# One decode step with cached attention: gate vectors in two halves, idle products over the whole array, and the softmax sums of a pair turned by a transposition

## The chip, the cores and the metric

The kernel runs on one core of a Trainium2 chip. The metric is device time in microseconds (us), as the median of repeated executions. A core has five engines that work side by side, each through its own queue of instructions in the order in which they were issued: TensorE (PE in the profile, its weight loads PEld), VectorE (DVE), ScalarE (ACT), GpSimd (POOL) and SyncE (SP, which here only issues transfers). Engines wait for one another through semaphores. Sixteen DMA engines move data between HBM and the on-chip memory SBUF; PE writes its results to PSUM.

## What is computed

One token goes through a block with adaptive layer norm: attention of one query over a cache, then a two-layer network with a squared ReLU.

```python
mod = (silu(c) @ w_mod).reshape(1, 6, 1, 640)        # c: (1, 640), w_mod: (640, 3840)
sa, ca, ga, sb, cb, gb = (mod[:, j] for j in range(6))
h = layernorm(x) * (1 + ca) + sa                      # x: (1, 1, 640)
q = (h @ wq).reshape(1, 1, 32, 192).transpose(0, 2, 1, 3)
scores = einsum("bhqd,bhkd->bhqk", q, k_cache) * 192 ** -0.5   # caches: (1, 32, 8192, 192)
o = einsum("bhqk,bhkd->bhqd", softmax(scores), v_cache)
x = x + ga * (o.reshape(1, 1, 6144) @ wo)
h = layernorm(x) * (1 + cb) + sb
x = x + gb * (relu(h @ w1 + b1) ** 2 @ w2 + b2)       # w1: (640, 1536), w2: (1536, 640)
```

Everything is in 32-bit floats. The two caches are 403 MB of the 452 MB that are read.

## The kernel before

**Slots and transfers.** SBUF has three large slots (`slot`), through which the caches and the weights pass in turn: for every head h the keys k (with the weights that the head's neighbours need behind them), then the values v. `load_k(h)` and `load_v(h)` stand at the top of the loop's pass over head h. SP issues a load as soon as the slot that it fills has been released: the keys of head h+1 go where the values of head h-1 were, the values of head h+1 where the keys of head h were. Behind the last values come `wm1_t` (the output weights of the last pair and three of the six modulation blocks), `w1_t` with the last modulation block `gb`, and `w2_t`, in the slots of the last heads.

**One head.** The 8192 positions lie 64 to each of 128 partitions. `keys` goes over the head's keys in two halves (head 31 in four quarters): DVE multiplies them by the query in place (L201), POOL adds part of the products in halves (L203), and DVE sums them to scores (L204, L205). After the first half, `between` issues either the query of the next pair (even heads) or the attention's output projection of the pair before (`attend`, odd heads). `softmax` takes the maximum over all positions, for which PE turns a column of 128 partial maxima (L220) and DVE reduces it (L222); ACT takes the exponential and, with it, the 128 partial sums of the head (L228), into a column of `sp`. `values` multiplies the probabilities with v on PE, in 24 products of 512 columns, three at a time, each in two passes (L240), into a PSUM tile of the tag "o".

**A pair of heads.** After an odd head's exponentials, `total` adds the partial sums of the pair's two heads over the partitions with a product by a matrix of ones (L97), which leaves the sums on every partition. `project(i - 1)` stands at the start of the odd head 2i+1: DVE takes the reciprocals (L213), then for each head of the pair picks the wanted entries out of the values' result, scaled by the reciprocal (L254), and adds them (L256); PE gathers the pair into one column (L258, `ps_oT`). `attend` later copies that to SBUF (L262, `oT`) and PE multiplies it by the output weights (L267, `att_a`; L272 for the last pair).

**The order.** The schedule is written by hand: each engine runs its instructions in the order of the program text. So on PE `project(i - 1)` stands behind the values of head 2i, and on DVE it stands ahead of `keys(2i + 1)`.

**Modulation.** `mod` computes blocks of the modulation on PE with the vector `e` (silu of c) repeated 32 times as the weights: for each of five blocks of rows four products (L140), one for each quarter of the 640 outputs, into the partitions of that quarter. So the result stands in 32 copies of 160 columns on each quarter of the partitions; DVE copies it to `mods` (L145). Block 2 (the gate `ga`) is computed between the softmax and the values of head 31, block 5 (the gate `gb`) after the first layer's product `ps_f` (L343).

**The tail.** `project(15)`, `attend(15)`, the residual `x1`, blocks 3 and 4 of the modulation, the layer norm, `ps_f`, the squared ReLU with its 32x32 transposition to `fT` (L82), block 5, the idle products `ps_warm` (L355), whose result nobody reads, and the second layer `ps_y` (L363), whose weights come in five pieces. DVE ends with the gate and the sum (L366, L367), and SP stores the result.

Of the kernel before, what the change touches and what calls it, by code (L numbers as in the profile page):

```python
# [8 lines left out]
F32 = mybir.dt.float32  # L9
AF = mybir.ActivationFunctionType  # L10
ALU = mybir.AluOpType
AX = mybir.AxisListType

P = 128
D = 640
# [4 lines left out]
G = 4  # L20
DG = D // G
FG = FF // G
KB = DG // 32
FB = FG // 32
PW = 2 * DH
E = 8
ED = 64
# [5 lines left out]
WO = 3 * D  # L33
# [12 lines left out]
def block_kernel(ctx: ExitStack, tc: tile.TileContext, kw, ky, vc, wm0, wm1, w1, gb, w2, out):  # L46
    nc = tc.nc
    const = ctx.enter_context(tc.tile_pool(name="const", bufs=1))
    strm = ctx.enter_context(tc.tile_pool(name="strm", bufs=3))
    work = ctx.enter_context(tc.tile_pool(name="work", bufs=2))  # L50
    psum = ctx.enter_context(tc.tile_pool(name="psum", bufs=1, space=bass.MemoryType.PSUM))
    ctx.enter_context(tc.manual_schedule())

    def slot(name):
        return strm.tile([P, SLOT], F32, tag="slot", name=name, bufs=3)


    ident = const.tile([P, P], F32, name="ident")
    make_identity(nc, ident)
    ones = const.tile([P, P], F32, name="ones")  # L60
    nc.vector.memset(ones, 1.0)

    mask = const.tile([P, E], F32, name="mask")
# [29 lines left out]
    def total(src, name):  # L93

        n = src.shape[1]
        ps = psum.tile([P, 512], F32, tag="sm", name="ps_" + name, bufs=2)
        nc.tensor.matmul(ps[:, :n], ones, src, start=True, stop=True)  # L97
        return ps[:, :n]
# [25 lines left out]
    e = const.tile([P, KB], F32, name="silu")  # L124
# [5 lines left out]
    mods = const.tile([P, 6, DG], F32, name="mods")  # L130

    def mod(first, n, w, steps=(KB,)):

        ps = psum.tile([P, 512], F32, tag="q", name=f"ps_mod{first}", bufs=2)
        b = 0
        for k in steps:
            for b in range(b, b + k):
                wb = w[:, b].rearrange("p (m n) -> p m n", m=n)
                for g in range(G):
                    nc.tensor.matmul(ps[32 * g:32 * (g + 1), :n * DG], e[:, b:b + 1].to_broadcast([P, 32]),  # L140
                                     wb[:, :, DG * g:DG * (g + 1)], start=(b == 0), stop=(b == KB - 1))
            b += 1
            if b < KB:
                yield
        nc.vector.tensor_copy(mods[:, first:first + n], ps[:, :n * DG].rearrange("p (m n) -> p m n", m=n))  # L145
        yield

    qb_t, k_t, v_t = {}, {}, {}

    def load(src, to, h, what):  # L150
# [6 lines left out]
    def load_k(h):  # L157

        load(kw[WITH_W.index(h)] if h in WITH_W else ky[WITHOUT_W.index(h)], k_t, h, "k")

    def load_v(h):
        load(vc[h], v_t, h, "v")
# [14 lines left out]
    def query(i, w):  # L177
        w = w.rearrange("p (b n) -> p b n", b=KB)
        ps = psum.tile([P, 512], F32, tag="q", name=f"ps_q{i}", bufs=2)
        for b in range(KB):  # L180
            nc.tensor.matmul(ps[:, :PW], hR[:, b], w[:, b], start=(b == 0), stop=(b == KB - 1))  # L181
        qb_t[i] = work.tile([P, PW], F32, name=f"qb{i}", tag="qb")
        nc.scalar.activation(qb_t[i], ps[:, :PW], AF.Copy, scale=DH ** -0.5)  # L183
# [24 lines left out]

    ri_t, ps_t, sum_t = {}, {}, {}

    def inverse(i):
        r = work.tile([P, 2], F32, tag="r", name=f"r{i}")
        nc.vector.reciprocal(r, sum_t.pop(i))  # L213
        ri_t[i] = r

    def softmax(h, sc):
        mp = work.tile([P, 1], F32, tag="mp", name=f"mp{h}")
        nc.vector.tensor_reduce(mp, sc, axis=AX.X, op=ALU.max)  # L218
        ps = psum.tile([P, 512], F32, tag="sm", name=f"ps_mx{h}", bufs=2)
        nc.tensor.transpose(ps[:, :P], mp.to_broadcast([P, P]), ident)  # L220
        nm = work.tile([P, 1], F32, tag="nm", name=f"nm{h}")
        nc.vector.tensor_reduce(nm, ps[:, :P], axis=AX.X, op=ALU.max, negate=True)  # L222

        p = work.tile([P, NPOS, 32 // E], F32, tag="p", name=f"p{h}", bufs=1)
        if h % 2 == 0:
            sum_t["part"] = work.tile([P, 2], F32, tag="sp", name=f"sp{h // 2}")
        sp = sum_t["part"]
        nc.scalar.activation(p, sc[:, :, None].to_broadcast([P, NPOS, 32 // E]), AF.Exp, bias=nm, accum_out=sp[:, h % 2:h % 2 + 1])  # L228
        if h % 2:
            sum_t[h // 2] = total(sp, f"sum{h // 2}")  # L230
        return p

    def values(h, p):
# [9 lines left out]
    os_t = {}  # L243

    def project(i):

        n = 32 * NV
        os_ = work.tile([P, 2, ED], F32, tag="os", name=f"os{i}")
        inverse(i)
        r2 = ri_t.pop(i)  # L250
        for a in range(2):
            h = 2 * i + a
            om = work.tile([P, ED, E], F32, tag="om", name=f"om{h}", bufs=1)
            nc.vector.scalar_tensor_tensor(om[:n], ps_t.pop(h)[:n].rearrange("p (d e) -> p d e", e=E), r2[:n, a:a + 1],  # L254
                                           mask[:n, None, :].to_broadcast([n, ED, E]), op0=ALU.mult, op1=ALU.mult)
            nc.vector.tensor_reduce(os_[:n, a], om[:n], axis=AX.X, op=ALU.add)  # L256
        os_t[i] = psum.tile([P, 512], F32, tag="sm", name=f"ps_oT{i}", bufs=2)
        nc.tensor.matmul(os_t[i][:, :n], os_[:n].rearrange("p a d -> p (a d)"), quad[:n], start=True, stop=True)  # L258

    def attend(i, w):  # L260
        oT = work.tile([P, 96], F32, tag="oT", name=f"oT{i}")
        nc.vector.tensor_copy(oT, os_t.pop(i)[:, :96])  # L262
        w = w.rearrange("p (j n) -> p j n", j=3)
        if i + 1 < NPAIR:
            for j in range(3):
                for g in range(2):
                    nc.tensor.matmul(att_a[32 * g:32 * (g + 1), :2 * DG], oT[:, 32 * j:32 * (j + 1)],  # L267
                                     w[:, j, 2 * DG * g:2 * DG * (g + 1)], start=(i == 0 and j == 0), stop=(i == NPAIR - 2 and j == 2))
            return
        for j in range(3):  # L270
            for g in range(G):
                nc.tensor.matmul(att_t[0][32 * g:32 * (g + 1), :DG], oT[:, 32 * j:32 * (j + 1)],  # L272
                                 w[:, j, DG * g:DG * (g + 1)], start=False, stop=(j == 2))

    def gather():

        nc.scalar.activation(att_s[:64], att_a[:64, :2 * DG], AF.Copy)
        att_t.append(psum.tile([P, 512], F32, tag="o", name="att", bufs=3))
        for g in range(G):
            nc.tensor.matmul(att_t[0][32 * g:32 * (g + 1), :DG], ident[:, 32 * (g // 2):32 * (g // 2) + 1].to_broadcast([P, 32]),  # L280
                             att_s[:, DG * (g % 2):DG * (g % 2 + 1)], start=True, stop=False)
# [3 lines left out]
    for h in range(H):  # L285
        i = h // 2
        if h:
            load_k(h)
        if h == H - 1:
            wm1_t = slot("wm1_t")  # L290
            nc.sync.dma_start(wm1_t[:, :WO + KB * D], wm1[:, :WO + KB * D])
        load_v(h)
        w = k_t[h][:, HD:]

        def between(c):
            if c == 0 and h % 2 and i:
                attend(i - 1, w)
            elif c == 0 and h % 2 == 0 and i + 1 < NPAIR:
                query(i + 1, w)
            elif c == 2 and h == H - 1:  # L300
                gather()

        if h % 2 and i:
            project(i - 1)
        sc = keys(h, between)
        p = softmax(h, sc)
        if h == H - 1:
            next(mod(2, 1, wm1_t[:, WO:WO + KB * D].rearrange("p (b n) -> p b n", b=KB)))
        values(h, p)


# [1 line left out]
    w1_t = slot("w1_t")  # L313
# [6 lines left out]
    gb_t = w1_t[:, KB * FF:KB * (FF + D)].rearrange("p (b n) -> p b n", b=KB)  # L320
    w1_t = w1_t[:, :KB * FF].rearrange("p (b n) -> p b n", b=KB)
    w2_t = w2_t[:, :FB * D].rearrange("p (b n) -> p b n", b=FB)

    project(NPAIR - 1)
    attend(NPAIR - 1, wm1_t[:, :WO])
    mod_b = mod(3, 2, wm1_t[:, WO + KB * D:WO + KB * 3 * D].rearrange("p (b n) -> p b n", b=KB), (2, 2, 1))
    next(mod_b)
# [13 lines left out]
    for b in range(KB):  # L341
        for g in range(G):
            nc.tensor.matmul(pf[32 * g:32 * (g + 1), :FG], hT2[:, b], w1_t[:, b, FG * g:FG * (g + 1)],  # L343
                             start=(b == 0), stop=(b == KB - 1))
    f = work.tile([P, FG], F32, name="f", tag="spread", bufs=1)
# [2 lines left out]
    nc.vector.tensor_mul(f, f, f)  # L348
    fT = columns(f, FG, "fT", work, tag="om", bufs=1)

    next(mod(5, 1, gb_t))
    idle = psum.tile([P, 512], F32, tag="sm", name="ps_warm", bufs=2)
    for k in range(WARM):
        for g in range(G):
            nc.tensor.matmul(idle[32 * g:32 * (g + 1)], ones[:, :32], w1_t[:, k, :512], start=True, stop=True)  # L355
    gb2 = const.tile([P, DG], F32, name="gb2")
    nc.vector.tensor_mul(gb2, mods[:, 5], bbt[:, FG:])
    nc.vector.tensor_add(x1, x1, gb2)
# [2 lines left out]
    for b in range(FB):  # L361
        for g in range(G):
            nc.tensor.matmul(py[32 * g:32 * (g + 1), :DG], fT[:, b], w2_t[:, b, DG * g:DG * (g + 1)],  # L363
                             start=(b == 0), stop=(b == FB - 1))
# [46 lines left out]
```

## Time and profile before

| | us |
|---|---|
| median of 3 executions | 1057.97 (1057.53 to 1058.03) |
| the profiled execution, whole time | 1057.63 |
| its span, first to last instruction | 1055.8 |
| DVE busy in the span | 831.4 |
| PE busy in the span | 451.2 |
| POOL busy in the span | 194.7 |
| ACT busy in the span | 33.4 |

The span is what the profile's times count from; the whole time also holds what lies around it, 1.8 us. In rows of a timeline the columns are: start, duration, engine, line of the kernel, operation, output from inputs, shapes, count; in brackets stands the idle time of the engine before the instruction, and what ended it. Rows of the groups have busy time and mean duration in nanoseconds after the bar. Rows of waits have the total, the number of times and the longest. Rows of transfers have the size of one, and the median time from issue to landing. A matmul of 32-bit floats has two records, one for each pass; a transposition has one.

```profile
PE 451.2 (43%) x2324; PEld 143.5 (14%) x2324; DVE 831.4 (79%) x409; ACT 33.4 (3%) x88; POOL 194.7 (18%) x72
```

### The profile page before, as it was taken

The page shows a single profiled execution, that of the slowest core. Times are in us where ns is not written, and L with a number is a line of the kernel's source. Part 1 is how long each engine was busy: PE and PEld are TensorE (multiplying, and loading weights), DVE is VectorE, ACT ScalarE, POOL GpSimd, SP SyncE. Part 2 cuts the span into 40 slices and gives each one's busy share as a digit, 9 for nine tenths or more (in the row PEclk, how much of TensorE's full clock was granted, in tenths as well). Part 3 has the DMA queues.
Part 4 walks back from the last instruction along what each step waited for, and adds up shares of the span by engine and source line. Part 5 has one row for each costly group of instructions (what it writes and reads, how often), then busy time and mean ns, then how long its engine had stood idle before and what let it go on. Part 6 is the DMA issues. An engine that isn't in the chain of part 4 may idle for free.

```text
span 1055.8 us, 5623 instructions
## 1 busy us (share of the span) xinstructions
PE 451.2 (43%) x2324; PEld 143.5 (14%) x2324; DVE 831.4 (79%) x409; ACT 33.4 (3%) x88; POOL 194.7 (18%) x72
## 2 busy tenths in 40 slices
PE   3235443344543344363334534335453334545446
PEld 1101111011111111020111111101111111111113
DVE  2886878978787987878888687987878798789963
ACT  1000000000000000000000000000000000000000
POOL 0211112211212221212221212221211221122110
PEclk9667656776665777666577666666666676666769
DMA  9999999999999999999999999999999999999997
GB/s 403 439 434 424 436 436 426 443 424 435 433 435 426 442 424 439 431 433 426 435 432 439 428 436 427 434 437 433 428 435 430 431 436 432 433 429 431 426 423 306
DMA packets 11409, 452.18 MB, mean 428 GB/s; under 512 B 1268, under 2 KB 1272, under 8 KB 1784
## 3 DMA queue, kind: packets, MB, share of 16 engines
q1 hardware_dynamic: 11384, 451.83, 99.3%
q8 instruction: 18, 0.29, 0.1%
q14 instruction: 7, 0.06, 0.0%
HBM read 451.82 MB, written 0.00 MB: 428 GB/s over the span
## 4 chain that ended last, share of the span: by engine, by line
DMA 42%; DVE 39%; PE 17%; ACT 1%; issue 1%; SPq 0%; DVEq 0%; ACTq 0%
DMA k<-in_kw 36%; DVE k L201 21%; PE ps_o L240 14%; DVE sc L204 12%; DVE sc L205 5%; DMA k<-in_ky 3%; DMA w_t<-in_w 2%; DMA wm_t<-in_wm 1%; ACT p L228 1%; PE ps_sum L97 1%; PE ps_mx L220 1%; PE ps_mod L140 1%; PE ps_q L181 0%; DVE nm L222 0%; DVE mp L218 0%
## 5 line engine op out<-in xcount | busy, mean ns | idle before, releaser
L201 DVE TENSOR_TENSOR k<-k,qb 128x6144 f32<-128x6144 f32 (+1 forms) x66 | 419.7, 6359 | 152.3 <-DMA k<-in_kw 148.0
L203 POOL TENSOR_TENSOR k<-k 128x1344 f32<-128x1344 f32 (+1 forms) x66 | 194.0, 2940 | 821.0 <-DVE k L201 443.9
L240 PE MATMUL ps_o<-v,p 128*32 128x512 f32 x1536 | 291.9, 734 | 17.2 <-ACT p L228 17.2
L204 DVE TENSOR_REDUCE sc<-k 128x18 f32<-128x3456 f32 (+1 forms) x66 | 240.5, 3644 | 4.3
L220 PE MATMUL ps_mx<-ident,mp 128*128 128x128 f32 x32 | 15.2, 474 | 421.7 <-DVE mp L218 421.7
L267 PE MATMUL att_a<-k,oT 128*32 128x320 f32 x180 | 49.5, 719 | 118.3 <-DVE oT L262 117.1
L205 DVE TENSOR_REDUCE sc<-k 128x14 f32<-128x1344 f32 (+1 forms) x66 | 99.0, 1500 | 0.0
L240 PEld LDWEIGHTS ps_o<-v,p 128*32 128x32 f32 x1536 | 68.7, 132 | 216.6 <-issue 194.3
L220 PEld LDWEIGHTS ps_mx<-ident,mp 128*128 128x128 f32 x32 | 5.8, 182 | 448.2 <-DVE mp L218 427.2
L181 PE MATMUL ps_q<-k,hR 128*128 128x384 f32 x150 | 52.4, 496 | 1.7 <-DMA k<-in_kw 1.7
L228 ACT ACTIVATE p<-sc,nm 128x256 f32<-128x256 f32 x32 | 16.2, 508 | 759.9 <-DVE nm L222 496.4
L267 PEld LDWEIGHTS att_a<-k,oT 128*32 128x32 f32 x180 | 13.7, 161 | 140.8 <-DVE oT L262 120.7
L181 PEld LDWEIGHTS ps_q<-k,hR 128*128 128x128 f32 x150 | 27.3, 190 | 29.9 <-issue 14.0
L254 DVE SCALAR_TENSOR_TENSOR om<-ps_o,r,mask 96x512 f32<-96x512 f32 x32 | 23.9, 747 | 7.0 <-PE ps_o L240 5.8
L222 DVE TENSOR_REDUCE nm<-ps_mx 128x1 f32<-128x128 f32 x32 | 9.3, 292 | 18.2 <-PE ps_mx L220 18.2
L256 DVE TENSOR_REDUCE os<-om 96x64 f32<-96x512 f32 x32 | 21.8, 682 | 1.1
L97 PE MATMUL ps_sum<-sp,ones 128*128 128x2 f32 x32 | 9.4, 364 | 17.2 <-ACT p L228 17.2
L140 PE MATMUL ps_mod<-wm_t,silu 128*32 128x320 f32 (+1 forms) x120 | 10.5, 503 | 14.5 <-DVE silu L128 14.5
L183 ACT ACTIVATE qb<-ps_q 128x384 f32<-128x384 f32 x16 | 7.8, 490 | 196.3 <-PE ps_q L181 196.3
L97 PEld LDWEIGHTS ps_sum<-sp,ones 128*128 128x128 f32 x32 | 8.0, 312 | 21.9 <-ACT p L228 21.9
L76 DVE COPY small<-wm_t 128x27 f32<-128x27 f32 x1 | 0.2, 179 | 11.1 <-DMA wm_t<-in_wm 11.1
L145 DVE COPY mods<-ps_mod 128x320 f32<-128x320 f32 (+1 forms) x4 | 1.6, 398 | 8.9 <-PE ps_mod L140 8.9
(77 smaller groups left out, 86.7 us busy)
## 6 DMA issues: line engine op xcount, KB each, us to landing
k<-in_kw SPq DMA_DIRECT2D x29, 7104.0 KB, 27.8
v<-in_vc SPq DMA_DIRECT2D x32, 6144.0 KB, 22.1
k<-in_ky SPq DMA_DIRECT2D x1, 6144.0 KB, 30.6
k<-in_ky SPq DMA_DIRECT2D x2, 3072.0 KB, 21.3
k<-in_kw SPq DMA_DIRECT2D x3, 1536.0 KB, 15.3
wm_t<-in_wm SPq DMA_DIRECT2D x1, 4173.5 KB, 12.6
wm_t<-in_wm SPq DMA_DIRECT2D x1, 3200.0 KB, 29.3
wm_t<-in_wm SPq DMA_DIRECT2D x1, 2560.0 KB, 18.4
```

What stands on the lines that cost most here:

```text
L97: nc.tensor.matmul(ps[:, :n], ones, src, start=True, stop=True)
L181: nc.tensor.matmul(ps[:, :PW], hR[:, b], w[:, b], start=(b == 0), stop=(b == KB - 1))
L201: nc.vector.tensor_mul(pr, pr, q[:, None, :].to_broadcast([P, n, DH]))
L203: nc.gpsimd.tensor_add(half, half, pr[:, m:, DH // 2:])
L204: nc.vector.tensor_reduce(s[:, :m], pr[:, :m], axis=AX.X, op=ALU.add)
L205: nc.vector.tensor_reduce(s[:, m:], half, axis=AX.X, op=ALU.add)
L220: nc.tensor.transpose(ps[:, :P], mp.to_broadcast([P, P]), ident)
L228: nc.scalar.activation(p, sc[:, :, None].to_broadcast([P, NPOS, 32 // E]), AF.Exp, bias=nm, accum_out=sp[:, h % 2:h % 2 + 1])
L240: nc.tensor.matmul(ps_t[h][32 * g:32 * (g + 1)], p[:, E * j:E * (j + 1)].rearrange("p e r -> p (e r)"), t[:, j, g], start=(j == 0), stop=( ...
L254: nc.vector.scalar_tensor_tensor(om[:n], ps_t.pop(h)[:n].rearrange("p (d e) -> p d e", e=E), r2[:n, a:a + 1], mask[:n, None, :].to_broadca ...
L256: nc.vector.tensor_reduce(os_[:n, a], om[:n], axis=AX.X, op=ALU.add)
L267: nc.tensor.matmul(att_a[32 * g:32 * (g + 1), :2 * DG], oT[:, 32 * j:32 * (j + 1)], w[:, j, 2 * DG * g:2 * DG * (g + 1)], start=(i == 0 an ...
```

## The change

Three things are changed; the transfers, the order of the heads and `keys` are not.

- **Gates.** Blocks 2 and 5 go through a new function `gate` in place of `mod`: the weights are 64 copies of `e`, and two products per block of rows, of 320 columns each, fill one half of the partitions each. ACT copies the four quarters to `mods`, each from the half and the columns in which it stands.
- **Idle products.** Two products with all 128 columns of ones in place of eight with 32.
- **Sums of a pair.** In place of the product with ones, ACT spreads the two columns of partial sums to 2 x 64 columns (`sx`). In `project` PE turns this by a transposition, so that the partial sums of head a stand on 64 partitions; at the end of `project` DVE adds them (`s`) and takes the reciprocal. The scaling by it moves from L254, which becomes a plain product, to the copy `oT`, which becomes a product with a scalar per partition.

```diff
+    def gate(i, w):
+
+        ps = psum.tile([P, 512], F32, tag="q", name=f"ps_mod{i}", bufs=2)
+        for b in range(KB):
+            for g in range(2):
+                nc.tensor.matmul(ps[64 * g:64 * (g + 1), :2 * DG], e[:, b:b + 1].to_broadcast([P, 64]),
+                                 w[:, b, 2 * DG * g:2 * DG * (g + 1)], start=(b == 0), stop=(b == KB - 1))
+        for g in range(G):
+            rows = slice(32 * g, 32 * (g + 1))
+            nc.scalar.activation(mods[rows, i], ps[rows, DG * (g % 2):DG * (g % 2 + 1)], AF.Copy)
...
-    def inverse(i):
-        r = work.tile([P, 2], F32, tag="r", name=f"r{i}")
-        nc.vector.reciprocal(r, sum_t.pop(i))
-        ri_t[i] = r
...
         if h % 2:
-            sum_t[h // 2] = total(sp, f"sum{h // 2}")
+            sum_t[h // 2] = work.tile([P, 2, ED], F32, tag="sx", name=f"sx{h // 2}", bufs=1)
+            nc.scalar.activation(sum_t[h // 2], sp[:, :, None].to_broadcast([P, 2, ED]), AF.Copy)
...
         os_ = work.tile([P, 2, ED], F32, tag="os", name=f"os{i}")
-        inverse(i)
-        r2 = ri_t.pop(i)
+
+        ps = psum.tile([P, 512], F32, tag="sm", name=f"ps_sum{i}", bufs=2)
+        nc.tensor.transpose(ps[:, :P], sum_t.pop(i).rearrange("p a c -> p (a c)"), ident)
         for a in range(2):
             h = 2 * i + a
             om = work.tile([P, ED, E], F32, tag="om", name=f"om{h}", bufs=1)
-            nc.vector.scalar_tensor_tensor(om[:n], ps_t.pop(h)[:n].rearrange("p (d e) -> p d e", e=E), r2[:n, a:a + 1],
-                                           mask[:n, None, :].to_broadcast([n, ED, E]), op0=ALU.mult, op1=ALU.mult)
+            nc.vector.tensor_mul(om[:n], ps_t.pop(h)[:n].rearrange("p (d e) -> p d e", e=E),
+                                 mask[:n, None, :].to_broadcast([n, ED, E]))
             nc.vector.tensor_reduce(os_[:n, a], om[:n], axis=AX.X, op=ALU.add)
         os_t[i] = psum.tile([P, 512], F32, tag="sm", name=f"ps_oT{i}", bufs=2)
         nc.tensor.matmul(os_t[i][:, :n], os_[:n].rearrange("p a d -> p (a d)"), quad[:n], start=True, stop=True)
+        s = work.tile([P, 1], F32, tag="s", name=f"s{i}")
+        nc.vector.tensor_reduce(s, ps[:, :P], axis=AX.X, op=ALU.add)
+        ri_t[i] = work.tile([P, 1], F32, tag="r", name=f"r{i}")
+        nc.vector.reciprocal(ri_t[i], s)
...
-        nc.vector.tensor_copy(oT, os_t.pop(i)[:, :96])
+        nc.vector.tensor_scalar(oT, os_t.pop(i)[:, :96], ri_t.pop(i), None, op0=ALU.mult)
...
-            next(mod(2, 1, wm1_t[:, WO:WO + KB * D].rearrange("p (b n) -> p b n", b=KB)))
+            gate(2, wm1_t[:, WO:WO + KB * D].rearrange("p (b n) -> p b n", b=KB))
...
-    next(mod(5, 1, gb_t))
+    gate(5, gb_t)
     idle = psum.tile([P, 512], F32, tag="sm", name="ps_warm", bufs=2)
     for k in range(WARM):
-        for g in range(G):
-            nc.tensor.matmul(idle[32 * g:32 * (g + 1)], ones[:, :32], w1_t[:, k, :512], start=True, stop=True)
+        nc.tensor.matmul(idle, ones, w1_t[:, k, :512], start=True, stop=True)
```

## The prediction, before the result was known

> **What bounds the kernel now.** Read first the page's chain and the use of the transfer engines, then what the queue of transfers (SP) waits for, then the timeline of one pair of heads, of the last three heads and of the tail.
>
> ```profile
> GB/s 403 439 434 424 436 436 426 443 424 435 433 435 426 442 424 439 431 433 426 435 432 439 428 436 427 434 437 433 428 435 430 431 436 432 433 429 431 426 423 306
> ...
> q1 hardware_dynamic: 11384, 451.83, 99.3%
> ...
> DMA 42%; DVE 39%; PE 17%; ACT 1%; issue 1%; SPq 0%; DVEq 0%; ACTq 0%
> ...
> SPq L155 <- DVE sc L205: 577.5, 29, 24.8
> SPq L155 <- PE ps_o L240: 260.8, 24, 12.0
> ```
>
> The chain names DMA, DVE and PE in turn, and SP's queue waits for DVE's keys and PE's values to free a slot. But the rate hardly moves between slices, about 434 GB/s, and the transfers fill 99.3% of 16 engines' span. So through the heads the stream of 452 MB sets the pace, and the other engines only have to free slots before it runs dry. How much room have they? One pair (heads 14 to 16; an odd head is the one in which `project` runs):
>
> ```profile
> 492.50 0.29 DVE L222 TENSOR_REDUCE nm<-ps_mx 128x1 f32<-128x128 f32 x1 [0.57 <-PE ps_mx L220]
> 492.70 0.16 DVE L213 RECIPROCAL r<-ps_sum 128x2 f32<-128x2 f32 x1
> 492.90 0.75 DVE L254 SCALAR_TENSOR_TENSOR om<-ps_o,r,mask 96x512 f32<-96x512 f32 x1
> ...
> 499.39 6.56 DVE L201 TENSOR_TENSOR k<-k,qb 128x6144 f32<-128x6144 f32 x1 [3.52 <-DMA k<-in_kw]
> ...
> 502.09 0.12 PEld L240 LDWEIGHTS ps_o<-v,p 128*32 128x32 f32 x3 [0.31 <-issue]
> ...
> 503.05 0.46 PE L258 MATMUL ps_oT<-quad,os 96*128 96x96 f32 x2
> ...
> 511.18 0.25 DVE L262 COPY oT<-ps_oT 128x96 f32<-128x96 f32 x1
> ...
> 511.48 3.41 PE L267 MATMUL att_a<-k,oT 128*32 128x320 f32 x12 [7.96 <-DVE oT L262]
> ...
> 523.20 0.33 SPq L155 DMA_DIRECT2D v<-in_vc  x1
> ...
> 530.71 6.56 DVE L201 TENSOR_TENSOR k<-k,qb 128x6144 f32<-128x6144 f32 x1 [6.46 <-DMA k<-in_kw]
> ```
>
> DVE starts an odd head at 499.39, after 3.52 us of waiting for its keys; PE is still in the values of the even head before it, and reaches the old `ps_oT` product (L258) only at 503.05. Today nothing on DVE waits for that, since the copy `oT` (L262) comes half a head later, at 511.18. The next even head starts at 530.71 after 6.46 us of waiting. So a late odd head has 6.46 us of cover. The load of the next v is issued at 523.20 and the one ahead of it lands at 530.7: 7.5 us of lead.
>
> **The change, part by part.** (1) *The sum turned by a transposition.* The transposition is issued in `project`, so in PE's queue it stands behind the values of the even head, where L258 stands now. DVE's new reduction `s` and the reciprocal are issued at the end of `project`, ahead of `keys`: the whole odd head, its multiply L201, its reductions and POOL's addition, is queued behind a wait for PE. The rows show this order being kept: in L213 (492.70) and L254 DVE runs `project` in the written order, and L262 waits for PE with L201 behind it (below, 999.08). The price: the transposition starts at 503.05; the nearest row for it is the one-pass transposition of the maximum, 474 ns (L220, quoted below); then 0.05 to reach DVE, 0.20 from a reduction of 128 columns to the next instruction (492.50 to 492.70), 0.20 from a reciprocal to the next (492.70 to 492.90). L201 starts 0.92 us after the L258 mark, at 503.97 in place of 499.39: 4.6 us later. Bounds for the hand-over: 0.46 us for two passes of L258 says a warm one-pass turn may take 0.25, and a wait that clears only after both PE products adds 0.46; so 0.7 to 1.4.
>
> In the middle this costs nothing as long as the cover lasts: 4.6 against 6.46 us, and the v load goes out at 527.8, 2.9 us ahead of 530.7. PE's even values start from an even head, which does not move, so the delay does not grow from pair to pair. Taken off there: 16 `ps_sum` products on PE (0.59 us each, the row at 1019.23 below); L254 loses its scalar and stays at or under its 0.75 us; DVE gains a reduction (0.29, the row at 492.50) per pair: all inside the same idle time. If the cover were gone, each of the 15 odd heads from head 3 on would cost its 4.6 us.
>
> (2) *Where the cover is gone: the last heads.*
>
> ```profile
> 939.43 6.56 DVE L201 TENSOR_TENSOR k<-k,qb 128x6144 f32<-128x6144 f32 x1 [3.56 <-DMA k<-in_kw]
> 943.22 0.46 PE L258 MATMUL ps_oT<-quad,os 96*128 96x96 f32 x2
> ...
> 964.22 6.55 DVE L201 TENSOR_TENSOR k<-k,qb 128x6144 f32<-128x6144 f32 x1
> ...
> 989.65 9.00 PE L240 MATMUL ps_o<-v,p 128*32 128x512 f32 x48 [1.08 <-ACT p L228]
> ...
> 991.90 3.35 DVE L201 TENSOR_TENSOR k<-k,qb 128x3072 f32<-128x3072 f32 x1
> ...
> 997.22 0.84 DVE L205 TENSOR_REDUCE sc<-k 128x7 f32<-128x672 f32 x1
> 998.58 0.30 PEld L258 LDWEIGHTS ps_oT<-quad,os 96*128 96x128 f32 x2 [0.84 <-DVE sc L205]
> 998.58 0.46 PE L258 MATMUL ps_oT<-quad,os 96*128 96x96 f32 x2
> ...
> 999.08 0.26 DVE L262 COPY oT<-ps_oT 128x96 f32<-128x96 f32 x1 [1.02 <-PE ps_oT L258]
> 999.25 3.35 DVE L201 TENSOR_TENSOR k<-k,qb 128x3072 f32<-128x3072 f32 x1
> ```
>
> Head 29: L201 moves from 939.43 to 943.22 + 0.92 = 944.14, 4.7 us later. Head 30 starts at 964.22 with no wait at all in front of it (its keys came early, and no `project` stands there), so all 4.7 us are handed on: its values end near 1003.3 in place of 998.6. Head 31 starts behind the second wait, at 998.58 + 4.7 + 0.92 = 1004.2 in place of 991.90. Its first quarter takes 6.16 us (991.90 to 997.22 + 0.84), then `oT`, and the second quarter starts near 1010.5 in place of 999.25: **11.25 us late**, because the wait of 1.02 us that `oT` has today is swallowed. From there to the end of head 31's keys nothing waits for transfers, so 11.25 us arrive whole at the softmax.
>
> (3) *The gates in halves, and the tail.*
>
> ```profile
> 1017.44 0.80 SPq L315 DMA_DIRECT2D w_t<-in_w  x2
> ...
> 1019.23 0.59 PE L97 MATMUL ps_sum<-sp,ones 128*128 128x2 f32 x2 [1.07 <-ACT p L228]
> ...
> 1019.75 2.89 PE L140 MATMUL ps_mod<-wm_t,silu 128*32 128x160 f32 x40
> ...
> 1022.42 7.98 PE L240 MATMUL ps_o<-v,p 128*32 128x512 f32 x48
> ...
> 1030.45 2.23 SPq L319 DMA_DIRECT2D w_t<-in_w  x5
> ...
> 1039.65 3.43 PE L343 MATMUL ps_f<-w_t,hT 128*32 128x384 f32 x40 [2.09 <-issue]
> ...
> 1042.87 1.57 PE L140 MATMUL ps_mod<-w_t,silu 128*32 128x160 f32 x40
> ...
> 1044.23 1.93 PE L355 MATMUL ps_warm<-w_t,ones 128*32 128x512 f32 x16
> ...
> 1044.72 0.58 DVE L82 STREAM_TRANSPOSE fT<-f 128x384 f32<-128x384 f32 x1
> ...
> 1047.35 1.84 PE L363 MATMUL ps_y<-w_t,fT 128*32 128x160 f32 x48 [1.19 <-DMA w_t<-in_w]
> ...
> 1051.98 0.48 PE L363 MATMUL ps_y<-w_t,fT 128*32 128x160 f32 x8 [0.32 <-DMA w_t<-in_w]
> ```
>
> A gate today: 40 records, four at a time, ten rounds of 160 columns: 2.89 us at the slow clock, 1.57 us at the fast one. In halves: 20 records, two at a time, ten rounds of 320 columns, so half the instructions and twice the streaming. The nearest row is the attention projection (511.48): 12 records of 320 columns, two at a time, six rounds in 3.41 us slow; half of that, 1.7, fast: 0.28 to 0.30 a round, 3.0 us fast. The value lies between 2.8 and, if two half-arrays do not run side by side, 6.0; I take 3.0, since the row shows two side by side.
>
> Gate 2 stands on PE between the softmax of head 31 and its values. Values that start on an idle PE take 9.00 us (989.65, above), those behind gate 2 7.98: part of PE's slow start is spent on the gate already. I take the slow stretch as a matter of time and not of work, so the added 1600 columns come out of fast time: +1.5 (at the slow rate +2.9); the `ps_sum` product that goes was slow, 0.59, worth 0.3. Values 31 end 11.25 + 1.2 = 12.45 us later, at about 1042.9. The four ScalarE copies have until the `x1` product 3 us later: ACT is idle there, and they take 0.43 us each at most (the 64x320 copy of L277, in the groups below).
>
> ```profile
> L220 PE MATMUL ps_mx<-ident,mp 128*128 128x128 f32 x32 | 15.2, 474 | 421.7 <-DVE mp L218 421.7
> ...
> L277 ACT ACTIVATE att_s<-att_a 64x320 f32<-64x320 f32 x1 | 0.4, 430 | 12.4 <-PE att_a L267 12.4
> ```
>
> From values 31 to the product `ps_f` the chain is as before (reduction and reciprocal fit beside the 0.46 us of L258; a scaled `oT` costs 0.25 to 0.30): `ps_f` starts at 1039.65 + 12.45 = 1052.1. Now PE is the late one: 3.22 us to gate 5 (1039.65 to 1042.87), gate 5 3.0 in place of 1.57, the idle products 1.93 (four records of 512 columns one after the other in place of four rounds of four: the same streaming), then all of `ps_y`. Today `ps_y` waits for w2 in four stretches; with w2 there, 96 records at 48 in 1.84 us take 3.7. End: 1052.1 + 3.22 + 3.0 + 1.93 + 3.7 = 1063.95 in place of 1051.98 + 0.48 = 1052.46: **+11.5 us**. `fT` is ready at 1045.30 + 12.45 = 1057.75, before the idle products end (1060.25): products that filled a wait now stand in the way, 2.5 us. Gate 5's copies (1.7 us) and 0.7 us for `gb2` and `x1` end near 1061, under `ps_y`.
>
> Is w2 there?
>
> ```profile
> wm_t<-in_wm SPq DMA_DIRECT2D x1, 4173.5 KB, 12.6
> wm_t<-in_wm SPq DMA_DIRECT2D x1, 3200.0 KB, 29.3
> ```
>
> The larger row is the kernel's first load: 12.6 us to landing, where 4173.5 KB at 434 GB/s are 9.85 us: a start-up of under 2.8. The other is the load ahead of w1, issued with v31 at about 999.1 (L312): it lands near 1028.4. w1 goes out at 1017.44 + 11.25 = 1028.7, so the stream may stand still for 2.8 us. w1 and gb (128 rows of 5·(1536+640) floats, 5.57 MB, 12.8 us) then land by 1044.3, w2 (128 rows of 12·640, 3.93 MB, 9.1 us) by about 1054, 6 us before `ps_y` starts. The stream no longer sets the end.
>
> **Sum.** The profiled execution took 1057.63 us with a span of 1055.8; 1057.63 + 11.5 = 1069.1. The median, 1057.97, is 0.34 above it: **1069.5**.
>
> **Rivals.** A measurement of this kernel can tell about 0.2% (2.1 us) from no change. (a) *Not slower:* the turned sum is ready before DVE asks, so that no odd head waits. It decides at 939.43 and 991.90: the transposition would have to run before the even head's values. Then 1.2 us for gate 2 and 1.5 for gate 5 delay PE: `ps_f` ends 1.2 later, `ps_y` starts near 1049.1 instead of 1047.35 and runs through to 1052.8, 0.35 late: 1058.3. Against it: the written order, which every row keeps. Chance 0.11. (b) *Half-arrays one after the other:* 3.0 us more in each gate, both on the path: 1075.5. For it: no row has this shape; against: the 32-wide pairs. Chance 0.07. (c) *A change of tile width stops the array.* L258 (full width, after 32-wide values) loads its weights after 0.84 us of idle loader where the value products show 0.31: 0.53 us. Gate 2 and the tail gain four such changes: +2.1, 1071.6. Against it: from L97 (full) to L140 (32) there is no gap at all. Chance 0.12. The Trainium skill, "TensorEngine Tiling (Array Packing)", section Tiling Modes, says that changing the tiling mode, not just the tile, drains TensorE; the first place agrees with its 0.53 us, the second does not show it, and by the page the time is this rival's. (d) *The stream runs dry in the odd heads:* with 2.9 us of lead left and a start-up of up to 2.8, a few pairs may lose up to 1 us: 1070 to 1083. Chance 0.05, since any such delay gives DVE its cover back. The forecast itself: 0.62. The remaining 0.03 is a gain that I don't see.
>
> **Range.** Below: if head 30 absorbed head 29's delay, 1069.5 - 4.7 = 1064.8, less 0.5 for two short hand-overs; above: rival (b), 1075.5. So 1064 to 1076, which leaves out (a), the gain, and part of (d). Faster 0.03, same 0.11, slower 0.86.
>
> **What would show it.** In odd heads DVE idles before L201 for some 8 us, released by PE's new transposition, not by DMA; before even heads the idle time falls from 6.46 to about 1.9; the average rate is unchanged up to 940 us; head 31's second quarter starts near 1010.5; gate 2 and gate 5 show 20 records each, gate 5 near 3.0 us; `ps_y` runs in one stretch with no wait for w2. The prediction is wrong if the idle before L201 still ends on DMA, if head 30 starts near 964, or if `ps_y` still waits for w2.

## The result and the profile after

The changed kernel takes **1075.19 us** (median of 6, 1071.31 to 1079.14) against 1057.91 us (6 executions, 1057.53 to 1058.03): a ratio of 1.0164, with a 95% interval of 1.0141 to 1.0187. The profiled execution took 1076.54 us, its span 1074.8. Forecast were 1069.5, from 1064 to 1076. The wait that was forecast is there, but the kernel loses half as much again as forecast (17.3 us for 11.5), half of it at a place where the forecast had nothing. The executions now differ by 8 us.

From the page of the changed kernel: the rate in 40 slices, the chain that ended last, and the groups of the keys' product (now L212) and of the new reduction (L268), with busy time, mean ns, and the idle time before them with what ended it.

```profile
GB/s 396 442 428 438 433 412 428 445 431 427 420 423 428 437 430 417 425 433 439 417 428 437 432 435 383 430 437 435 435 408 430 432 435 429 425 417 407 441 396 208
...
DVE 41%; DMA 38%; PE 19%; ACT 1%; issue 1%; DVEq 0%
...
L212 DVE TENSOR_TENSOR k<-k,qb 128x6144 f32<-128x6144 f32 (+1 forms) x66 | 419.7, 6359 | 56.8 <-DMA k<-in_kw 49.3
...
L268 DVE TENSOR_REDUCE s<-ps_sum 128x1 f32<-128x128 f32 x16 | 4.6, 290 | 111.8 <-PE ps_sum L258 111.8
```

The keys' product in the page of the kernel before:

```profile
L201 DVE TENSOR_TENSOR k<-k,qb 128x6144 f32<-128x6144 f32 (+1 forms) x66 | 419.7, 6359 | 152.3 <-DMA k<-in_kw 148.0
```

DVE now stands still for 111.8 us in front of 16 reductions, waiting for PE's transposition (L258), and its waits for the keys are down from 148.0 to 49.3 us. That is the wait of the prediction. The first row tells more: slices of 383 to 425 GB/s stand among those of 427 to 445. Before, only the first slice and the last two were under 424.

A pair in the timeline of the changed kernel, heads 14 to 16:

```profile
497.97 8.94 PE L247 MATMUL ps_o<-v,p 128*32 128x512 f32 x48 [1.02 <-ACT p L234]
...
506.84 0.33 PE L258 MATMUL ps_sum<-ident,sx 128*128 128x128 f32 x1
...
507.20 0.29 DVE L268 TENSOR_REDUCE s<-ps_sum 128x1 f32<-128x128 f32 x1 [7.17 <-PE ps_sum L258]
507.53 0.16 DVE L270 RECIPROCAL r<-s 128x1 f32<-128x1 f32 x1
507.61 6.56 DVE L212 TENSOR_TENSOR k<-k,qb 128x6144 f32<-128x6144 f32 x1
...
531.48 0.33 SPq L166 DMA_DIRECT2D v<-in_vc  x1
...
535.04 6.56 DVE L212 TENSOR_TENSOR k<-k,qb 128x6144 f32<-128x6144 f32 x1 [2.50 <-DMA k<-in_kw]
...
593.46 0.33 SPq L166 DMA_DIRECT2D v<-in_vc  x1
600.56 6.56 DVE L212 TENSOR_TENSOR k<-k,qb 128x6144 f32<-128x6144 f32 x1 [6.08 <-DMA k<-in_kw]
...
636.04 0.29 DVE L268 TENSOR_REDUCE s<-ps_sum 128x1 f32<-128x128 f32 x1 [8.04 <-PE ps_sum L258]
...
660.32 0.33 SPq L166 DMA_DIRECT2D v<-in_vc  x1
663.15 6.56 DVE L212 TENSOR_TENSOR k<-k,qb 128x6144 f32<-128x6144 f32 x1 [1.78 <-DMA k<-in_kw]
```

DVE is ready early, but the reduction starts only when the even values and the turn behind them are through (506.84 + 0.33), after 7.17 us, and the odd head's product follows 0.41 us later. The even head still waits for its keys: 2.50 us of the old 6.46. But look at the pairs: head 16 starts at 535.04, head 18 at 600.56, head 20 at 663.15. One pair takes 65.5 us, the next 62.6, which is the old pace. (Some of the 65.5 is not new: in the kernel before, the pair from head 16 to head 18 took 64.0.) The load of the next v goes out 3.56, 7.10 and 2.83 us before the keys ahead of it have landed. Behind a short lead a long pair follows, behind a long lead a short pair. The windows around the load at 660.32 show what happens (a window counts a transfer packet, with all of its time, where the packet starts; columns: stretch, length, busy time of PE, its weight loads, DVE, ACT and POOL with counts, granted clock, share of the DMA engines, GB/s):

```profile
655.00:657.00 2.00, 0.00 (x0) 0.00 (x0) 1.97 (x2) 0.00 (x0) 1.91 (x1) 0.60 1.05 455
657.00:659.00 2.00, 0.00 (x0) 0.00 (x0) 2.00 (x2) 0.00 (x0) 1.11 (x1) 0.50 0.53 227
659.00:661.00 2.00, 0.44 (x1) 0.18 (x1) 1.47 (x2) 0.00 (x0) 0.00 (x0) 0.50 0.07 28
661.00:663.00 2.00, 0.92 (x7) 0.23 (x9) 0.29 (x1) 0.91 (x3) 0.00 (x0) 0.50 1.33 393
```

From 657 fewer packets start, and from 659 to 661 almost none. A packet of this load takes 2.1 us, so the engines fall idle some 2 us after the share falls: by the packets' own times in the trace they are all busy until 658.5, then on the mean for 0.28 of the time from 659 to 661, and for nearly all of it again from 661.5. The trace has sixteen completions for this load of keys, as many as there are engines, and the number of busy engines falls with them: the first at 659.09, the eighth at 659.53, the last at 663.07. The next load is issued only at 660.32. So the time of landing, for which DVE waits until 663.15, is that of the last of 16 engines; half of them are done 3.5 us before it and have nothing to do until the next load comes.

The last heads and the tail, in the changed kernel's timeline:

```profile
916.77 6.56 DVE L212 TENSOR_TENSOR k<-k,qb 128x6144 f32<-128x6144 f32 x1 [2.29 <-DMA k<-in_kw]
...
951.17 0.29 DVE L268 TENSOR_REDUCE s<-ps_sum 128x1 f32<-128x128 f32 x1 [6.95 <-PE ps_sum L258]
951.58 6.56 DVE L212 TENSOR_TENSOR k<-k,qb 128x6144 f32<-128x6144 f32 x1
...
976.41 6.55 DVE L212 TENSOR_TENSOR k<-k,qb 128x6144 f32<-128x6144 f32 x1
...
1012.10 3.36 DVE L212 TENSOR_TENSOR k<-k,qb 128x3072 f32<-128x3072 f32 x1
...
1018.41 3.35 DVE L212 TENSOR_TENSOR k<-k,qb 128x3072 f32<-128x3072 f32 x1
...
1036.84 0.47 PE L226 MATMUL ps_mx<-ident,mp 128*128 128x128 f32 x1 [13.58 <-DVE mp L224]
...
1037.24 4.80 PE L153 MATMUL ps_mod<-wm_t,silu 128*64 128x320 f32 x20
...
1037.74 0.51 ACT L234 ACTIVATE p<-sc,nm 128x256 f32<-128x256 f32 x1 [15.29 <-DVE nm L228]
...
1041.97 7.07 PE L247 MATMUL ps_o<-v,p 128*32 128x512 f32 x48
...
1049.09 2.23 SPq L331 DMA_DIRECT2D w_t<-in_w  x5
...
1051.43 1.83 PE L284 MATMUL att<-wm_t,oT 128*32 128x160 f32 x24 [0.41 <-DVE oT L274]
...
1059.89 3.43 PE L355 MATMUL ps_f<-w_t,hT 128*32 128x384 f32 x40 [2.25 <-DVE hT L82]
...
1063.26 2.91 PE L153 MATMUL ps_mod<-w_t,silu 128*64 128x320 f32 x20
...
1066.10 1.99 PE L366 MATMUL ps_warm<-w_t,ones 128*128 128x512 f32 x4
...
1068.01 3.47 PE L374 MATMUL ps_y<-w_t,fT 128*32 128x160 f32 x96
```

One row of the kernel before is still needed, the start of head 28:

```profile
908.10 6.56 DVE L201 TENSOR_TENSOR k<-k,qb 128x6144 f32<-128x6144 f32 x1 [6.45 <-DMA k<-in_kw]
```

Against the rows of before, the delay of the profiled execution adds up as follows. Each line is the difference of two starts, less the delay that is already there.

| place | before | after | delay | added | forecast |
|---|---|---|---|---|---|
| head 28 starts | 908.10 | 916.77 | 8.67 | 8.67 | 0 |
| head 29 starts | 939.43 | 951.58 | 12.15 | 3.48 | 4.7 |
| head 30 starts | 964.22 | 976.41 | 12.19 | 0.04 | 0 |
| head 31, second quarter | 999.25 | 1018.41 | 19.16 | 6.97 | 6.55 |
| w2 issued (values 31 done) | 1030.45 | 1049.09 | 18.64 | -0.52 | 1.2 |
| `ps_f` starts | 1039.65 | 1059.89 | 20.24 | 1.60 | 0 |
| `ps_y` ends | 1052.46 | 1071.48 | 19.02 | -1.22 | -0.95 |

### The profile page after: what moved, and what is told of

Read it like the earlier page. It is cut to its first block, busy times and chain, and to the rows that moved or that the text cites. A ratio compares the mean times of both kernels' runs of the same rounds, so it can differ in the third digit from the quotient of the medians.

```text
span 1074.8 us, 5528 instructions
## 1 busy us (share of the span) xinstructions
PE 450.3 (42%) x2256; PEld 138.7 (13%) x2256; DVE 833.1 (78%) x423; ACT 40.7 (4%) x112; POOL 194.9 (18%) x72
## 4 chain that ended last, share of the span: by engine, by line
DVE 41%; DMA 38%; PE 19%; ACT 1%; issue 1%; DVEq 0%
DMA k<-in_kw 37%; DVE k L212 22%; PE ps_o L247 14%; DVE sc L215 13%; DVE sc L216 5%; DMA wm_t<-in_wm 1%; ACT p L234 1%; PE ps_mod L140 1%; PE ps_mx L226 1%; PE ps_mod L153 1%; PE ps_q L192 1%; DVE nm L228 0%; DVE mp L224 0%; PE ps_y L374 0%; PE ps_f L355 0%
## 5 line engine op out<-in xcount | busy, mean ns | idle before, releaser
L212 DVE TENSOR_TENSOR k<-k,qb 128x6144 f32<-128x6144 f32 (+1 forms) x66 | 419.7, 6359 | 56.8 <-DMA k<-in_kw 49.3
L268 DVE TENSOR_REDUCE s<-ps_sum 128x1 f32<-128x128 f32 x16 | 4.6, 290 | 111.8 <-PE ps_sum L258 111.8
L262 DVE TENSOR_TENSOR om<-ps_o,mask 96x512 f32<-96x512 f32 x32 | 21.8, 681 | 10.7 <-PE ps_o L247 10.1
L140 PE MATMUL ps_mod<-wm_t,silu 128*32 128x320 f32 x80 | 9.7, 638 | 15.0 <-DVE silu L128 15.0
L224 DVE TENSOR_REDUCE mp<-sc 128x1 f32<-128x64 f32 x32 | 7.0, 220 | 1.1
L192 PE MATMUL ps_q<-wm_t,hR 128*128 128x384 f32 x10 | 6.2, 806 | 1.9 <-DVE hR L186 1.9
```

Of the source, the lines that this page charges most:

```text
L212: nc.vector.tensor_mul(pr, pr, q[:, None, :].to_broadcast([P, n, DH]))
L262: nc.vector.tensor_mul(om[:n], ps_t.pop(h)[:n].rearrange("p (d e) -> p d e", e=E), mask[:n, None, :].to_broadcast([n, ED, E]))
```

## The experiments

Two theories stand against each other. The **wait theory**: everything comes from DVE's wait in `project`, at the end through the chain of heads 29 to 31, and in the middle because the late odd head sends the next load of v too late, so that the stream runs dry. Its rivals: the gates and idle products cost the time; or the loss in the middle has another cause (PE's or DVE's new work, DVE standing still) than the late load. Times are medians; ratios go against executions of the kernel before on the same chip (1057.74 to 1057.83).

### The wait taken away

The reduction and its reciprocal move from the end of `project` to `attend`, half a head later (as a function `inverse`):

```diff
     def attend(i, w):
+        inverse(i)
         oT = work.tile([P, 96], F32, tag="oT", name=f"oT{i}")
```

> The changed kernel, with one thing moved: the reduction and the reciprocal stand in attend, directly ahead of the copy oT, and no longer in project ahead of the keys. If DVE's wait for PE's transposition is the whole cost (the 8.7 us lost by head 28 and the 10.5 lost in heads 29 and 31 alike), the time returns to 1057 to 1059. If the gates in halves or the full-width idle products cost something on the path, it stays above by that: 1060 or more. If the loss by head 28 comes from anything else in the change (PE's or ACT's new work), it stays near 1066.

Measured: 1058.00 us (11 executions, 1057.52 to 1061.13), ratio 1.0008 (0.9999 to 1.0017). In this kernel's waits (total us, times, longest) nearly nothing is left of the wait for the turned sums, and the keys' product waits for its keys again:

```profile
DVE k L212 <- DMA k<-in_kw: 143.9, 29, 7.8
...
DVE s L271 <- PE ps_sum L258: 0.9, 1, 0.9
```

So the whole loss, middle and end, hangs on where DVE's two small instructions stand.

In the second version they stay in `project`, and PE's transposition is taken out of it (`turn`) and issued ahead of the even head's values:

```diff
+        if h % 2 == 0 and i:
+            turn(i - 1)
         values(h, p)
```

> The changed kernel, with PE's transposition issued ahead of the even head's values and not behind them; reduction and reciprocal stay in project. This is the rival of the prediction that would not be slower. If the place in PE's queue is the cause, DVE finds the sums ready and the time is 1057 to 1059. If the reduction itself or its wait costs something wherever the transposition stands, it stays above 1062.

Measured: 1057.89 us (11 executions, 1057.60 to 1058.96), ratio 1.0002 (0.9994 to 1.0011). Its timeline for heads 14 and 15:

```profile
495.87 0.28 DVE L274 TENSOR_REDUCE s<-ps_sum 128x1 f32<-128x128 f32 x1
496.18 0.16 DVE L276 RECIPROCAL r<-s 128x1 f32<-128x1 f32 x1
...
499.80 6.56 DVE L212 TENSOR_TENSOR k<-k,qb 128x6144 f32<-128x6144 f32 x1 [3.46 <-DMA k<-in_kw]
...
502.61 0.46 PE L272 MATMUL ps_oT<-quad,os 96*128 96x96 f32 x2
```

The same reduction now runs at 495.87 without a wait, and the odd head waits for its keys as before. The reduction itself costs nothing; its place behind PE's 9 us of values did.

### The parts of the change

The gates in halves and the full-width idle products alone, on the kernel before (the diff's `gate` functions, calls and idle loop; the sums untouched):

> The kernel before with the gates in halves and the full-width idle products alone; the sums as before. By the wait theory these parts cost only the tail: gate 2 behind the sums' product +1.2 to +1.5, gate 5 +1.4, two or three changes of width at 0.5 each, less the 1.2 us that the last product waits for w2 today: 1059 to 1061. The rival that the gates cause the loss would give 1065 or more.

Measured: 1060.39 us (11 executions, 1059.29 to 1060.88), ratio 1.0021 (1.0013 to 1.0030). And the turned sums alone, with the gates and idle products of before:

> The changed kernel with the gates and the idle products of before: only the turned sums are left. By the wait theory nearly the whole loss stays: 1072 to 1075. By the gate theory 1058 to 1062.

Measured: 1071.08 us (4 executions, 1069.14 to 1072.19), ratio 1.0123 (1.0109 to 1.0136), 1 us under the stretch expected. The sums carry 13.3 of the 17.3 us; the gates and idle products cost 2.6 alone, and some 4 in the changed kernel, with a spread of some us in both.

### The middle and the end apart

The reduction in `project` for the pairs whose `project` runs in heads 3 to 27 (`i < 13`), or for heads 29 and 31 alone (`13 <= i < 15`), otherwise in `attend`:

> As the mended kernel (reduction in attend), but with the reduction left in project for the pairs whose project runs in heads 3 to 27: only the middle waits. If late loads of v let the stream run dry there, the time is 8 us above the mended one: 1064 to 1068, with the rate falling just behind every second load of v. If the middle is covered, as the prediction's sum has it, 1057 to 1059, and the loss by head 28 needs another cause.

> The other half: the reduction in project in heads 29 and 31 only. The prediction's chain (head 29 hands its delay to 30, 31 waits again) gives 10 to 11 us above the mended kernel: 1067 to 1070. If the loss at the end arises only because the stream is already late, 1058 to 1062.

Measured: the middle alone 1066.89 us (4 executions, 1065.14 to 1068.40), ratio 1.0082 (1.0065 to 1.0098); the end alone 1068.05 (4 executions, 1065.85 to 1068.32), ratio 1.0094 (1.0079 to 1.0109). Against the mended kernel, which ran on another chip (the kernel before differs by 0.1 us between the two), these are 8.9 and 10.1 us: two losses of like size, and each arises without the other (their sum, 19.0, is a little more than the 17.3 of both together). The chain through the last heads, which the prediction worked out, is there with its size; the middle, which it set at nothing, is the other half.

### A late load of v by itself

Does the late load starve the stream, or something else in the odd head's delay? In the kernel before, POOL gets an addition on the keys that have just been used, which the v load into that slot has to wait for. No other engine waits for anything new. A second run has 896 columns in place of 1792.

```diff
+        if h % 2 == 0 and 4 <= h <= 28:
+            late = k_t[h - 1][:, :1792]
+            nc.gpsimd.tensor_add(late, late, late)
         load_v(h)
```

> The kernel before, with an addition by POOL on 1792 columns of the odd head's used keys (some 3.9 us) ahead of the load of v in the even heads 4 to 28, so that this load goes out 4 us later; DVE, PE and ACT wait for nothing new. If the lead of the v load is what counts, the stream runs dry as in the changed kernel: 1062 to 1068, in every second pair. If DVE's standing still is what counts, 1057 to 1059.

> The same with 896 columns, some 2 us. The lead is then about 5.5 us in place of 7.5. If there is a threshold between the 5 to 6 us of the pairs that ran full in the changed kernel and the 3 us of those that ran dry, nothing is lost: 1057 to 1059. If every microsecond of lateness costs its share, 1060 to 1063.

Measured: 1057.73 us (10 executions), ratio 1.0000 (0.9991 to 1.0010), and 1057.85 (10 executions), 1.0001 (0.9992 to 1.0010). Neither put the question. The timeline of the first:

```profile
521.25 3.17 POOL L294 TENSOR_TENSOR k<-k 128x1792 f32<-128x1792 f32 x1
...
524.45 0.33 SPq L155 DMA_DIRECT2D v<-in_vc  x1
...
530.99 6.56 DVE L201 TENSOR_TENSOR k<-k,qb 128x6144 f32<-128x6144 f32 x1 [6.43 <-DMA k<-in_kw]
```

The addition started while DVE was still busy with the keys, and the load went out only 1 us later, 6.54 us ahead of the landing in place of 7.51; in the second run it hardly moved. So all that follows is that a lead of 6.5 us costs nothing. So once more, with the columns that DVE reads last, 2304 of them, and in a further run twice on 1792:

```diff
-            late = k_t[h - 1][:, :1792]
+            late = k_t[h - 1][:, HD - 2304:HD]
```

> The two runs with late v loads before this one did not do what they were meant to: POOL's addition did not touch the columns that DVE reads last, so it began before the keys were done, and the lead fell only from 7.5 to 6.5 us or not at all. Now the addition works on the last 2304 columns, which DVE reads last (some 4 us): the v load of the even heads 4 to 28 goes out 4 us later, with a lead of about 3.4 us as in the changed kernel, and no compute engine waits for anything new. If the lead alone starves the stream: 1062 to 1068 and a fall of the rate behind these loads in every second pair. If DVE's standing still does it in another way: 1057 to 1059.

> The same with two additions on the last 1792 columns, some 6.3 us: a lead of about 1 us. By the lead theory more is lost per pair, but the even head's keys then land later and give lead back: between the loss of the 4 us version and 13 pairs times 2.5 us more, 1066 to 1095. By the other theory 1057 to 1059.

Measured: 1068.91 us (4 executions, 1067.54 to 1070.64), ratio 1.0106 (1.0092 to 1.0120), and 1086.60 (4 executions, 1085.62 to 1086.93), ratio 1.0271 (1.0257 to 1.0285). Timeline and windows of the first:

```profile
530.00 4.02 POOL L295 TENSOR_TENSOR k<-k 128x2304 f32<-128x2304 f32 x1 [2.22 <-DVE sc L205]
...
534.05 0.33 SPq L155 DMA_DIRECT2D v<-in_vc  x1
537.97 6.56 DVE L201 TENSOR_TENSOR k<-k,qb 128x6144 f32<-128x6144 f32 x1 [6.93 <-DMA k<-in_kw]
...
1059.71 1.84 PE L367 MATMUL ps_y<-w_t,fT 128*32 128x160 f32 x48 [1.21 <-DMA w_t<-in_w]
```

```profile
531.00:533.00 2.00, 1.22 (x5) 0.70 (x8) 0.04 (x1) 0.60 (x2) 2.00 (x1) 0.50 1.01 426
533.00:535.00 2.00, 2.00 (x12) 0.50 (x9) 0.00 (x0) 0.00 (x0) 1.02 (x1) 0.50 0.38 150
```

The load goes out at 534.05, 3.92 us before the keys ahead of it have landed. From 533 to 535 few packets start; by the packets' own times the engines are busy for 0.77 of the time from 534.5 to 536, where the kernel before has no gap at all. DVE waits its 6.93 us for the keys as before, PE's second layer still waits for w2 (1059.71), and yet the kernel takes 11.2 us longer: 0.86 us on the mean for each of 13 late loads (leads of 3 to 5 us), and 2.2 in the second run (leads of 1 to 2.7). A late load alone makes a loss like that of the middle, and the odd head's delay is only the way to it. The expected stretch (to 1068) was passed by 1 us; and the loss fell on more pairs than every second one, since here nothing but the load's own lateness sets the lead.

The traces also show from where the lead has to be counted: from the moment at which the first of the sixteen engines has finished the load ahead, and not from the landing. Take the loads of v in heads 4 to 28 in the profiles of all 13 kernels, 169 loads, and the engines' mean idle time from 4 us before each issue to 6 us after it. Each of the loads issued up to 1.6 us before the first completion, or after it, left the engines idle, for 0.10 to 2.84 us. None of those issued 1.75 us or more before it left them idle for more than 0.04. Counted from the landing there is no such border: in the first of these two runs one load lost 0.77 us with a lead of 5.0, another 0.02 with a lead of 3.9, because there the engines finished within 4.85 and within 2.1 us of each other.

### Without the idle products

The mended kernel without the products that nobody reads:

```diff
-    for k in range(WARM):
-        nc.tensor.matmul(idle, ones, w1_t[:, k, :512], start=True, stop=True)
```

> The mended kernel (reduction in attend) without the idle products, whose result nobody reads. If they stand in the way of the second layer when PE is late, as its profile shows (1.98 us directly ahead of it), the runs above 1058 come down and the median is 1057.5 to 1058.0. If they keep PE's clock up, the second layer's products run at half speed: 1059 to 1062.

Measured: 1057.99 us (11 executions, 1057.73 to 1058.92), ratio 1.0003 (0.9994 to 1.0012). The median stays, the slowest execution falls from 1061.13 to 1058.92. That the idle products made the slow executions is not shown: the two kernels ran on different chips, and in the profile of the mended kernel (1059.12 us) the granted clock is 0.5 for 3.4 us in the tail, from 1034.7, while in that of this run (1057.88 us) it stays at 1.0 there. No version tried beats the kernel before.

## Why the prediction was right, and where it was short

The way of the loss in the last heads was forecast; the loss in the middle was not. That the time still lies between 1064 and 1076 is in part luck: the upper end was set for half-arrays that run one after the other, which they don't, and without the middle the kernel would have stayed under the forecast, at 1068.05 in the run with the end alone.

**The wait (step 1): right.** L201's successor starts an odd head 0.77 us after the turn begins (506.84 to 507.61; forecast 0.92), and taking away nothing but the wait gives the time back (1058.00, 1057.89). The rival (a), the turn ahead of the values, is the kernel that was then run.

**"In the middle this costs nothing as long as the cover lasts": wrong.** This is the step that failed, and with it the 0.05 given to rival (d). It measured 8.67 us in the profile and 8.9 in the run with the middle alone. The cover was counted at DVE, where it did last (2.50 us of idle time were left). It was also counted at the v load: a lead of 2.9 us against a start-up of under 2.8 was taken to be enough, as if all engines ran to the moment of landing. They don't: at head 16 of the kernel before the first engine is done 2.4 us before the landing, at head 20 4.1 us, at head 20 of the changed kernel 4.0 us. The runs with a late load alone show no loss at 6.5 us of lead, 0.86 us a load at 3 to 5, and 2.2 at 1 to 2.7. So the sign that the rate would not change up to 940 us failed: from 100 to 900 us it is 428 GB/s on the mean for 433. What rival (d) said of itself is right: the late keys give lead back, so in the changed kernel only every second load is late enough to leave the engines idle.

**The last heads (step 2): right.** Head 29's delay goes to head 30 in full (12.15, 12.19), and head 31 waits again; 3.48 and 6.97 us for 4.7 and 6.55, together 10.5 for 11.25, and 10.1 in the run with the end alone.

**Gate 2 (step 3): wrong in sign, -0.52 for +1.2.** The prediction kept it behind the exponentials, where it stood because the sums' product ahead of it waited for them. With that product gone it waits for nothing of the softmax: it starts at 1037.24, ahead of the exponentials (1037.74), and runs beside them. With the sums as before, the gates in halves and the full-width idle products cost 2.6 us; that run's profile has the fall of the clock told of next as well, so the 2.6 are not the place of gate 2 alone.

**From the values to `ps_f`: 1.60 for 0.** The chain is the same, but PE ran at half its clock through a part of it, as the windows of the changed kernel and of the kernel before show (the granted clock is the third number from the end):

```profile
1052.00:1053.00 1.00, 1.00 (x20) 0.73 (x16) 0.00 (x0) 0.00 (x0) 0.00 (x0) 0.50 0.76 282
1053.00:1054.00 1.00, 1.00 (x12) 0.38 (x8) 0.57 (x2) 0.00 (x0) 0.00 (x0) 0.50 0.98 394
```

```profile
1032.40:1033.40 1.00, 0.65 (x21) 0.59 (x24) 0.26 (x1) 0.00 (x0) 0.00 (x0) 1.00 0.99 418
```

Two rows of the timeline of the kernel before go with them:

```profile
1032.79 1.02 PE L272 MATMUL att<-wm_t,oT 128*32 128x160 f32 x24 [0.35 <-DVE oT L262]
...
1033.63 1.26 PE L140 MATMUL ps_mod<-wm_t,silu 128*32 128x320 f32 x16
```

The projection `att` took 1.83 us (1051.43, above) for 1.02, the modulation behind it 2.10 for 1.26: 1.65 us together, and so all of the 1.60. What sets the moment of that change was not tried. A fall to 0.5 for 3.4 us between the end of the values and gate 5 stands in the profiles of five of the seven kernels with the gates in halves, and of none of the six with the gates of before.

**The tail: right.** From the start of `ps_f` to the end of `ps_y` 11.59 us for 11.85: gate 5 takes 2.91 (forecast 3.0), the idle products 1.99 (1.93), `ps_y` in one stretch 3.47 (3.7), with w2 there. So rival (b) fell: two half-arrays run side by side. Of rival (c), 0.53 us at each change of width, next to nothing is to be seen: 3.37 us from `ps_f` to gate 5 (3.22 before), 2.84 on to the idle products, 1.91 on to `ps_y`, no more than their own lengths. The 0.84 us from which the price was taken is idle time of the weight loader alone; PE's products follow one another there without a gap (the row of the values ends at 989.65 + 9.00 = 998.65, L258 starts at 998.58). The Trainium skill, "TensorEngine Tiling (Array Packing)", section Tiling Modes, has a drain at such a change; if there is one here, it is too short to be seen in these starts.

In sum, the forecast of 11.5 us was short of the profile's 19.0 by 7.5: 8.67 in the middle and 1.60 of clock, less 1.72 at gate 2, 0.8 in the last heads and 0.27 in the tail.

## What to carry to other kernels

A small instruction that waits for another engine's queue holds up everything behind it on its own engine: place it behind the work that doesn't need its result, or place its producer ahead of the other engine's long block; either gave all of it back here. Where a stream of transfers sets the pace, the idle time of the compute engines is not the cover that counts: ask when the first transfer engine has finished the load ahead, and issue the next one at least a start-up before that (here 1.75 us), since the landing is that of the last engine and may come several us later. Count instructions last: 68 products and as many weight loads fewer on TensorE (2256 for 2324) bought nothing.

## What the hardware showed that was not expected

Sixteen engines share a load and don't finish it together: in the kernel before, the completions of one load of keys lie 2.4 us apart at head 16 and 4.1 us at head 20, with the stream full all the time. So the lead that the next 6 MB load needs, counted from the landing, is not one number; counted from the first completion it lay between 1.6 and 1.75 us, over all kernels tried. With the wait in it, the kernel's executions spread over 8 us; those of the kernel before over 0.5.
